# One GpSimd queue for all stores and zero fills, SyncE for loads alone, and more homes for w_mod tiles in a decode layer's forward and backward

## The chip, the core, the metric

The kernel runs on one core of a Trainium2 chip. A core has five engines that run on their own (TensorE for matmuls, VectorE, ScalarE, GpSimd, SyncE) and 16 DMA engines between HBM and the on-chip memory. The metric is the device time of one execution in microseconds; smaller is better. The runs come from several chips; the kernel before, run beside each group of them, took 719.1 to 720.5 us in the median, so times from different chips may be compared to within about 1 us.

## The reference

A decode layer for one token: adaptive layernorm, attention over a window of 4096 cached keys, a gated feed-forward, and the gradients of all of it.

```python
mod = (silu(c) @ w_mod).reshape(1, 6, 1, 1024)      # sa, ca, ga, sb, cb, gb
h = layernorm(x) * (1 + ca) + sa
x = x + ga * attention(h, k_cache[last 4096 of 65536], v_cache[same], wq, wo)
h = layernorm(x) * (1 + cb) + sb
x = x + gb * ((sigmoid(h @ w_gate) * (h @ w_up)) @ w_down)
# returned: x, and the gradients of x, k_cache, v_cache, wq, wo, w_gate, w_up, w_down, c, w_mod
```

With one token, each weight gradient is an outer product as large as its weight. The gradients of the two caches cover all 65536 positions, of which 61440 are zero: 120 MiB of zeros, written in 120 transfers of 1 MiB ("zero fills"). So 265.7 MB move, 186 of them written, and the arithmetic is small.

## The kernel before

Everything lives in one on-chip arena. Weight tiles are changed in place: VectorE reduces a tile against a broadcast gradient, then an outer product overwrites the tile, then the tile is stored. A tile's place is free for the next load only when its store has landed.

Zero fills go out on GpSimd's queue and are paced: each is tied to some result, so that they spread over the run.

```python
def zero(n, after=None):
    for _ in range(n):
        if not zleft:
            return
        ins = nc.gpsimd.dma_start(out=zleft.pop(0), in_=zeros[:, :])
        if after is not None:
            dep(ins, after)                 # wait for that result
```

The feed-forward (FFN) loop, seven blocks, five places for tiles ("slots"):

```python
def slot(i):
    return ar(F_OFF + 8 * (i % 5), 8)
wd_t = [slot(3 * n) for n in range(NB)]       # w_down; w_up: 3n+1; w_gate: 3n+2
...                                           # (cut)
for n in range(NB):
    ...                                       # (cut) gate and up matmuls (they need wu, wg), sigmoid,
    ...                                       # dhh = wd . b1k, ffn matmuls, dug, broadcast to du_b, dg_b
        outer_dve(wd[:, jj, :], hh[:, jj:jj + 1], b1k)
    nc.sync.dma_start(out=wd_dram(out_8, n), in_=wd_t[n])
    for j in range(KD):
        ttr(wu[:, j, :], wu[:, j, :], du_b, dh2acc[:, n * 16 + j:n * 16 + j + 1])
        last = outer_act(wu[:, j, :], h2[:, j:j + 1], du_b)
    nc.scalar.dma_start(out=dwu_view[:, :, n * FB:(n + 1) * FB], in_=wu)
    zero(1, last)
    if n + 1 < NB:
        if n + 1 > 1:
            load_wd(n + 1)
        load_wu(n + 1)
    ...                                       # (cut) the same for wg, stored by ScalarE, zero(1, last)
    if n + 1 < NB:
        load_wg(n + 1)                        # its slot is wd's of this block
```

A tile of w_up or w_gate is 128 partitions by 8 rows of 1 KB ("narrow rows"); w_down tiles and zero fills have rows of 8 KB. In the attention backward, w_mod is loaded again in eight tiles, into only two places:

```python
def sec_tile(j):
    return ar(F_OFF + 24 + 8 * (j % 2), 8)
```

## Time and profile before

| | before |
|---|---|
| time, median of 3 runs (lowest to highest) | 719.91 us (718.37 to 722.34) |
| span of the profiled run | 718.1 us |
| DMA busy, mean of 16 engines | 93% (42.2 + 37.9 + 13.1 + 0.2) |
| VectorE / ScalarE / TensorE / GpSimd busy | 43 / 29 / 21 / 9% |
| mean FFN block (first to seventh gate matmul, divided by 6) | 30.7 us |

One more part of the page is the DMA queues: packets, megabytes, and the share of the 16 engines' time that their packets took. q0 is GpSimd's queue, q1 SyncE's, q10 ScalarE's.

```profile
q0 software_dynamic: 17280, 125.84, 42.2%
q1 hardware_dynamic: 29920, 103.82, 37.9%
q10 hardware_dynamic: 21136, 35.66, 13.1%
```

The reader is to see the ratio of bytes to packets: GpSimd's queue moves 125.84 MB in 17280 packets, 7.3 KB each (8 KB and some for signalling), while ScalarE's moves 1.7 KB a packet, as two thirds of its packets are narrow rows (14336 of 1 KB).

### The profile page before, as it was taken

To read this page: it belongs to the slowest core of one execution; us is meant where nothing else is said; L and a number is where in the kernel's file an instruction comes from. 1 tells how busy PE (TensorE), PEld (TensorE's weight loads), DVE (VectorE), ACT (ScalarE), POOL (GpSimd) and SP (SyncE) were. 2 spreads that over 40 slices of the span, in tenths; PEclk is the share of its full clock that TensorE was granted. 3 is DMA by queue.
4 is the path that set the end of the run, shared out by engine and by line. 5 is a ranking of instruction groups with operands and counts; after the bars stand their busy time and mean duration, and the time that the engine had idled before them with its cause. 6 is when DMAs were issued, how large, how long until landed. Compare 5 with 4: busy or idle time off the path is not lost.

```text
span 718.1 us, 6808 instructions
## 1 busy us (share of the span) xinstructions
PE 148.1 (21%) x2648; PEld 125.4 (17%) x2648; DVE 309.3 (43%) x610; ACT 208.7 (29%) x298; POOL 66.1 (9%) x128
## 2 busy tenths in 40 slices
PE   2221226651220110201011100407714220000000
PEld 2221214551220110201011100106513120000000
DVE  2000003600236828356381899403994363200676
ACT  1000004610115606154260772445713230000026
POOL 2001101120100000000000021102100110000000
PEclk9999999965555555555555555556555555555555
DMA  8999999999969788797968699999999999997896
GB/s 347 428 426 425 427 425 427 416 421 416 417 251 377 273 321 309 270 365 249 381 209 325 241 412 422 398 407 419 416 420 425 413 418 417 412 422 281 323 384 270
DMA packets 68367, 265.74 MB, mean 370 GB/s; under 512 B 4208, under 2 KB 32880, under 8 KB 43120
## 3 DMA queue, kind: packets, MB, share of 16 engines
q0 software_dynamic: 17280, 125.84, 42.2%
q1 hardware_dynamic: 29920, 103.82, 37.9%
q10 hardware_dynamic: 21136, 35.66, 13.1%
q8 instruction: 20, 0.33, 0.2%
q14 instruction: 11, 0.09, 0.0%
HBM read 79.70 MB, written 185.60 MB: 369 GB/s over the span
## 4 chain that ended last, share of the span: by engine, by line
DMA 69%; DVE 16%; PE 6%; ACT 5%; issue 2%; SPq 1%; ACTq 1%; DVEq 0%
DMA out_dram<-arena 25%; DMA arena<-in_B_w_gate_dram 19%; DMA arena<-in_w_mod_dram 8%; DVE arena L151 8%; DMA arena<-in_A_wq_dram 6%; DMA arena<-in_A_k_cache_dram 5%; DMA arena<-in_A_wo_dram 4%; ACT arena L155 4%; DVE junk L151 2%; DVE arena L147 2%; PE tp_kv L309 2%; PE bc_ps L208 1%; ACT arena L312 1%; PE gu_ps L440 1%; DVE mx L330 1%
## 5 line engine op out<-in xcount | busy, mean ns | idle before, releaser
L151 DVE CUSTOM_DVE_ANT_0 arena<-arena 128x4096 bf16<-128x4096 bf16 (+1 forms) x24 | 88.5, 3709 | 97.0 <-DMA arena<-in_w_mod_dram 96.8
L119 POOL DMA_DIRECT2D out_dram<-zeros x120 | 65.0, 543 | 627.8 <-ACT arena L155 148.1
L440 PE MATMUL gu_ps<-h_bf,arena 128*128 128x1 bf16 x448 | 16.9, 172 | 152.0 <-DMA arena<-in_B_w_up_dram 102.5
L155 ACT ACTIVATE arena<-arena,cs_col 128x2048 bf16<-128x2048 bf16 x8 | 16.0, 2002 | 108.9 <-DVE dcs L151 106.4
L155 ACT ACTIVATE arena<-b1k,o_col 128x1024 bf16<-128x1024 bf16 x32 | 34.4, 1138 | 38.3 <-issue 15.5
L312 ACT COPY arena<-tp_kv 128x1024 bf16<-128x1024 bf16 x13 | 13.1, 1010 | 106.7 <-PE tp_kv L309 106.7
L440 PEld LDWEIGHTS <-arena 128*128 128x128 bf16 x448 | 16.0, 117 | 154.1 <-issue 131.5
L134 DVE TENSOR_TENSOR hh<-sg,gu_ps 128x4 f32<-128x4 f32 x7 | 1.1, 158 | 88.3 <-ACT om L445 88.3
L151 DVE CUSTOM_DVE_ANT_0 arena<-arena,b1k 128x1024 bf16<-128x1024 bf16 x32 | 36.7, 1217 | 0.0
L151 DVE CUSTOM_DVE_ANT_0 arena<-arena,du_b 128x512 bf16<-128x512 bf16 x56 | 34.8, 686 | 3.1 <-ACT du_b L473 3.1
L155 ACT ACTIVATE arena<-dg_b,h 128x512 bf16<-128x512 bf16 x56 | 35.0, 708 | 3.7 <-DVE dh2acc L151 3.7
L155 ACT ACTIVATE arena<-du_b,h 128x512 bf16<-128x512 bf16 x56 | 34.9, 710 | 0.0
L151 DVE CUSTOM_DVE_ANT_0 arena<-arena,dg_b 128x512 bf16<-128x512 bf16 x56 | 34.8, 685 | 0.0
L151 DVE CUSTOM_DVE_ANT_0 junk<-arena,b1k 128x1024 bf16<-128x1024 bf16 x28 | 34.2, 1222 | 0.5
L444 ACT ACTIVATE sg<-gu_ps 128x4 f32<-128x4 f32 x7 | 1.2, 173 | 93.3 <-PE gu_ps L440 93.3
L613 ACT ACTIVATE arena<-ps_kv 128x512 bf16<-128x512 f32 x32 | 16.1, 627 | 41.6 <-DMA out_dram<-arena 40.7
L309 PE MATMUL tp_kv<-ident_bf,arena 128*128 128x128 bf16 x256 | 22.3, 254 | 23.5 <-DMA arena<-in_A_k_cache_dram 15.6
L143 DVE COPY arena<-tp_kv 128x1024 bf16<-128x1024 bf16 x19 | 13.0, 690 | 31.0 <-PE tp_kv L309 31.0
L162 PE MATMUL rp_dc<-ident_f,dcv 128*8 128x128 f32 x1 | 0.4, 377 | 123.1 <-DVE dcv L134 123.1
L607 PE MATMUL ps_kv<-Q_hd,arena 8*128 8x128 bf16 x128 | 16.1, 295 | 41.6 <-ACT arena L613 41.6
L309 PEld LDWEIGHTS <-arena 128*128 128x128 bf16 x256 | 19.4, 116 | 26.3 <-DMA arena<-in_A_k_cache_dram 16.5
L162 PEld LDWEIGHTS rp_dc<-ident_f,dcv 128*8 128x8 f32 x1 | 0.1, 84 | 123.5 <-DVE dcv L134 123.5
(171 smaller groups left out, 336.3 us busy)
## 6 DMA issues: line engine op xcount, KB each, us to landing
out_dram<-zeros POOLq DMA_DIRECT2D x120, 1024.0 KB, 18.1
out_dram<-arena ACTq DMA_DIRECT2D x30, 1024.0 KB, 19.0
out_dram<-arena SPq DMA_DIRECT2D x23, 1024.0 KB, 18.7
arena<-in_A_wq_dram SPq DMA_DIRECT2D x15, 1024.0 KB, 40.4
arena<-in_w_mod_dram SPq DMA_DIRECT2D x8, 1536.0 KB, 26.9
arena<-in_A_wo_dram SPq DMA_DIRECT2D x8, 1024.0 KB, 37.7
arena<-in_w_mod_dram SPq DMA_DIRECT2D x8, 1024.0 KB, 5.8
arena<-in_B_w_down_dram SPq DMA_DIRECT2D x7, 1024.0 KB, 9.1
```

Source lines behind the costliest of these rows:

```text
L119: ins = nc.gpsimd.dma_start(out=zleft.pop(0), in_=zeros[:, :])
L143: return nc.vector.tensor_copy(out=out, in_=a)
L147: return nc.vector.tensor_scalar(out=out, in0=a, scalar1=s1, scalar2=None, op0=op0)
L151: return nc.vector.tensor_tensor_reduce(out=out, in0=w, in1=b, scale=1.0, scalar=0.0, op0=ALU.mult, op1=ALU.add, accum_out=acc)
L155: return nc.scalar.activation(out=out, in_=b, func=ACT.Copy, scale=col)
L208: nc.tensor.matmul(ps[:, jj * P:(jj + 1) * P], lhsT=col_bf[:, j0 + jj:j0 + jj + 1].broadcast_to([P, P]), rhs=ident_bf[:, :], start=(jj == ...
L309: nc.tensor.transpose(tp[:, t8 * P:(t8 + 1) * P], src[:, g, t_ * DH:(t_ + 1) * DH], ident_bf[:, :])
L312: last = nc.scalar.copy(out=o, in_=tp[:, :])
L330: nc.vector.reduce_max(out=mx8[:, ch:ch + 1], in_=P_bf[:, ch * 512:(ch + 1) * 512], axis=AX.X)
L440: nc.tensor.matmul(gu[:, half * 4 + jj:half * 4 + jj + 1], lhsT=w[:, j, jj::4], rhs=h2_bf[:, j:j + 1], start=(j == 0), stop=(j == KD - 1))
L607: nc.tensor.matmul(ps[:, t4 * DH:(t4 + 1) * DH], lhsT=rows[32 * g:32 * g + HG, t_ * P:(t_ + 1) * P], rhs=hd[32 * g:32 * g + HG, :], start= ...
L613: last = nc.scalar.activation(out=o, in_=ps[:, :], func=ACT.Copy, scale=float(scale))
```

## The change

The intent: no transfer should wait in the middle of a queue of another kind. All stores and zero fills go to GpSimd in one fixed order; SyncE only loads; ScalarE issues no transfers. (Exceptions of a few KB: three output vectors still leave by SyncE, and ScalarE still loads three input vectors at the start.) In the FFN loop each store is followed by two zero fills, so 42 are written there in place of 21, and w_down and w_up are loaded a block earlier. In the backward, each of the eight w_mod tiles (and of the eight half-size ones) has a place of its own in memory that has become free.

```diff
+    ZF = [(2, 2, 2)] * NB          # zero fills behind the wd, wu, wg store of a block
+    ZW_ = [1, 1, 1, 1, 1, 1, 1, 6] # behind the wo stores; ZS w_mod, ZQ wq, ZK k/v, ZT end
...
     load_wd(1)
+    load_wu(1)
...
-        last = cp(dug_bf, dug)
-        zero(1, last)
...
-        nc.sync.dma_start(out=wd_dram(out_8, n), in_=wd_t[n])
+        nc.gpsimd.dma_start(out=wd_dram(out_8, n), in_=wd_t[n])
+        zero(ZF[n][0])
...
-        nc.scalar.dma_start(out=dwu_view[:, :, n * FB:(n + 1) * FB], in_=wu)
-        zero(1, last)
-        if n + 1 < NB:
-            if n + 1 > 1:
-                load_wd(n + 1)
-            load_wu(n + 1)
+        nc.gpsimd.dma_start(out=dwu_view[:, :, n * FB:(n + 1) * FB], in_=wu)
+        zero(ZF[n][1])
...
-        nc.scalar.dma_start(out=dwg_view[:, :, n * FB:(n + 1) * FB], in_=wg)
-        zero(1, last)
+        nc.gpsimd.dma_start(out=dwg_view[:, :, n * FB:(n + 1) * FB], in_=wg)
+        zero(ZF[n][2])
         if n + 1 < NB:
             load_wg(n + 1)
+        if n + 2 < NB:
+            load_wd(n + 2)
+            load_wu(n + 2)
...
-    def sec_tile(j):
-        return ar(F_OFF + 24 + 8 * (j % 2), 8)
+    sec_off = [F_OFF + 24, F_OFF + 32, A_OFF + 56, C_OFF + 16, C_OFF + 24, B_OFF, B_OFF + 8, B_OFF + 16]
+    sec_t = [ar(o, 8) for o in sec_off]
+    s2_off = [B_OFF + 24, B_OFF + 28, F_OFF + 24, F_OFF + 28, F_OFF + 32, F_OFF + 36, A_OFF + 56, A_OFF + 60]
...            # (cut) all stores of the backward to nc.gpsimd with zero fills behind them, loads moved up,
...            # k/v gradient tiles alternate between two places, outputs of x and x2 moved to the end
```

More of the change, by code (lines that the diff above doesn't have):

```diff
@@ L113, in dep @@
                           reason="pace")
+    ZF = [(2, 2, 2)] * NB
+    ZW_ = [1, 1, 1, 1, 1, 1, 1, 6]
+    ZS = [1, 1, 1, 1, 1, 1, 1, 1]
+    ZQ = [1, 1, 1, 1, 1, 1, 1, 1]
+    ZK = [0, 0, 1, 0, 1, 0, 1, 0]
+    ZT = [0] * 7 + [99]
     def zero(n, after=None):
@@ L341, with transpose_rows @@
     zero(2, last)
-    def transpose_rows(src, name):
+    def transpose_rows(src, name, engs="AVAV"):
         dst = pool.tile([P, KT, G, HG], BF16, name=name, tag="pTdsT")
@@ L351, in transpose_rows @@
             i = tp[:, :].rearrange("p (t g r) -> p t g r", t=8, g=G)[:, :, :, 0:HG]
-            if tb % 2 == 0:
+            if engs[tb] == "A":
                 nc.scalar.copy(out=o, in_=i)
@@ L512 @@
     last = mulv(dmod_bf[:, 16:24], dx1, attn_col)
-    zero(4, last)
+    zero(2)
     dS = ar(F_OFF, 8)
@@ L520, with sec, s2_load @@
     dcs = vt([P, 2 * KD], "dcs")
-    def sec_tile(j):
-        return ar(F_OFF + 24 + 8 * (j % 2), 8)
+    sec_off = [F_OFF + 24, F_OFF + 32, A_OFF + 56, C_OFF + 16, C_OFF + 24, B_OFF, B_OFF + 8, B_OFF + 16]
+    sec_t = [ar(o, 8) for o in sec_off]
+    s2_off = [B_OFF + 24, B_OFF + 28, F_OFF + 24, F_OFF + 28, F_OFF + 32, F_OFF + 36, A_OFF + 56, A_OFF + 60]
+    s2_t = [ar(o, 4) for o in s2_off]
     def sec_load(j):
-        nc.sync.dma_start(out=sec_tile(j), in_=wm_view[:, j, 2048:6144])
-    def sec_ttr(j):
-        ttr(sec_tile(j), sec_tile(j), dmod_b4, dcs[:, j:j + 1])
-    def sec_outer(j, eng):
-        if eng == "A":
-            last = outer_act(sec_tile(j), cs_col[:, j:j + 1], dmod_b4)
-        else:
-            last = outer_dve(sec_tile(j), cs_col[:, j:j + 1], dmod_b4)
-        nc.sync.dma_start(out=dwm_view[:, j, 2048:6144], in_=sec_tile(j))
-        return last
+        nc.sync.dma_start(out=sec_t[j], in_=wm_view[:, j, 2048:6144])
+    def sec(j, nz):
+        ttr(sec_t[j], sec_t[j], dmod_b4, dcs[:, j:j + 1])
+        outer_dve(sec_t[j], cs_col[:, j:j + 1], dmod_b4)
+        nc.gpsimd.dma_start(out=dwm_view[:, j, 2048:6144], in_=sec_t[j])
+        zero(nz)
+    def s2_load(j):
+        nc.sync.dma_start(out=s2_t[j], in_=wm_view[:, j, 0:2048])
     sec_load(0)
     sec_load(1)
+    bcast(dmod_bf[:, 16:48], 32, dmod_b4, "A")
     do_col = vt([P, HQ], "do_col")
@@ L549 @@
             ttr(w, w, dattn_b, do_col[:, h:h + 1])
-            last = outer_act(w, o_col[:, h:h + 1], dattn_b)
-        nc.scalar.dma_start(out=dwo_view[:, q4 * 4:(q4 + 1) * 4, :], in_=wo_t[q4])
-        zero(2, last)
-    x2 = vt([P, KD], "x2")
-    mulv(x2, gb, ffn)
-    addv(x2, x2, x1)
-    col_to_row_out(x2, out_0[0], "x2")
-    for j in range(1, KD):
-        nc.sync.dma_start(out=wq_t[j], in_=wq_view[:, j, :])
+            outer_act(w, o_col[:, h:h + 1], dattn_b)
+        nc.gpsimd.dma_start(out=dwo_view[:, q4 * 4:(q4 + 1) * 4, :], in_=wo_t[q4])
+        zero(ZW_[q4])
+        if q4 < 7:
+            nc.sync.dma_start(out=wq_t[q4 + 1], in_=wq_view[:, q4 + 1, :])
+    sec_load(2)
     do_col2 = vt([P, 2 * HQ], "do_col2", BF16)
@@ L578 @@
                              tile_position=(0, 32 * g))
-        last = nc.vector.scalar_tensor_tensor(out=dS[:, ch * 512:(ch + 1) * 512], in0=ps[:, :], scalar=crow[:, 0:1],
-                                              in1=P_bf[:, ch * 512:(ch + 1) * 512], op0=ALU.subtract, op1=ALU.mult)
-    zero(2, last)
-    dsT = transpose_rows(dS, "dsT")
+        nc.vector.scalar_tensor_tensor(out=dS[:, ch * 512:(ch + 1) * 512], in0=ps[:, :], scalar=crow[:, 0:1],
+                                       in1=P_bf[:, ch * 512:(ch + 1) * 512], op0=ALU.subtract, op1=ALU.mult)
+    sec_load(3)
+    sec_load(4)
+    dsT = transpose_rows(dS, "dsT", "AAAA")
     DO_hd = make_hd(do_col2, "DO_hd")
-    bcast(dmod_bf[:, 16:48], 32, dmod_b4, "A")
+    sec(0, ZS[0])
     dq_ps, mm = av_like(k_nat, dsT, "dq")
-    zero(2, mm)
+    sec_load(5)
+    sec_load(6)
+    sec_load(7)
     dq_bf = vt([P, HQ], "dq_bf", BF16)
     ts(dq_bf, dq_ps[:, 0:HQ], SCALE, ALU.mult)
-    last = bcast(dq_bf, HQ, dq_b, "AV")
-    zero(2, last)
+    bcast(dq_bf, HQ, dq_b, "A")
+    sec(1, ZS[1])
+    for j in range(6):
+        s2_load(j)
     def kv_out(og, g):
@@ L596, with grad_kv @@
     gkv = []
-    for rows, hd, og, dst, scale in ((P_bf, DO_hd, out_3, x_T, None), (dS, Q_hd, out_2, k_nat, SCALE)):
+    for k, (rows, hd, og, scale) in enumerate(((P_bf, DO_hd, out_3, None), (dS, Q_hd, out_2, SCALE))):
         for g in range(G):
+            dst = ar(C_OFF + 8 * (g % 2), 8)
             for tb in range(KT // 4):
                 gkv.append((rows, hd, og, dst, scale, g, tb))
-    def grad_kv(items):
+    def grad_kv(items, nz):
         for rows, hd, og, dst, scale, g, tb in items:
@@ L608, in grad_kv @@
                                  rhs=hd[32 * g:32 * g + HG, :], start=True, stop=True, tile_position=(32 * g, 0))
-            o = dst[:, g, tb * 512:(tb + 1) * 512]
+            o = dst[:, tb * 512:(tb + 1) * 512]
             if scale is None:
-                last = nc.scalar.copy(out=o, in_=ps[:, :])
+                nc.scalar.copy(out=o, in_=ps[:, :])
             else:
-                last = nc.scalar.activation(out=o, in_=ps[:, :], func=ACT.Copy, scale=float(scale))
+                nc.scalar.activation(out=o, in_=ps[:, :], func=ACT.Copy, scale=float(scale))
             if tb == KT // 4 - 1:
-                nc.scalar.dma_start(out=kv_out(og, g), in_=dst[:, g, :])
-                zero(1, last)
+                nc.gpsimd.dma_start(out=kv_out(og, g), in_=dst)
+                zero(nz)
     dh1 = vt([P, KD], "dh1")
@@ L622 @@
         ttr(wq_t[j], wq_t[j], dq_b, dh1[:, j:j + 1])
-        grad_kv(gkv[8 * j:8 * j + 8])
-        last = outer_dve(wq_t[j], h1[:, j:j + 1], dq_b)
-        nc.sync.dma_start(out=dwq_view[:, j, :], in_=wq_t[j])
-        zero(1, last)
-        if j % 2 == 1 and j < 6:
-            k = j // 2
-            sec_ttr(k)
-            last = sec_outer(k, "V")
-            zero(1, last)
-            sec_load(k + 2)
+        outer_dve(wq_t[j], h1[:, j:j + 1], dq_b)
+        nc.gpsimd.dma_start(out=dwq_view[:, j, :], in_=wq_t[j])
+        zero(ZQ[j])
+        grad_kv(gkv[8 * j:8 * j + 8], ZK[j])
+        if j % 2 == 1:
+            sec(2 + j // 2, ZS[2 + j // 2])
+            if j == 1:
+                s2_load(6)
+                s2_load(7)
     dln1 = vt([P, KD], "dln1")
     mulv(dln1, dh1, ca1)
+    cp(dmod_bf[:, 0:8], dh1)
+    mulv(dmod_bf[:, 8:16], dh1, ln1)
+    dmod_b2 = dS[:, 0:2048]
+    bcast(dmod_bf[:, 0:16], 16, dmod_b2, "A")
     dx0b = layernorm_bwd_col(dln1, ln1, rstd1, "ln1b")
@@ L639 @@
     addv(dx0, dx0b, dx1)
-    cp(dmod_bf[:, 0:8], dh1)
-    last = mulv(dmod_bf[:, 8:16], dh1, ln1)
-    zero(2, last)
-    dmod_b2 = dS[:, 0:2048]
-    bcast(dmod_bf[:, 0:16], 16, dmod_b2, "A")
-    col_to_row_out(dx0, out_1[0], "dx0")
-    s2_t = [ar(C_OFF + 4 * j, 4) for j in range(KD)]
-    for j in range(KD):
-        nc.sync.dma_start(out=s2_t[j], in_=wm_view[:, j, 0:2048])
-    for k in range(3, KD):
-        sec_ttr(k)
-        last = sec_outer(k, "V")
-        zero(2, last)
-        if k + 2 < KD:
-            sec_load(k + 2)
-    zero(200, last)
+    col_to_row_out(dx0, out_1[0], "dx0")
+    x2 = vt([P, KD], "x2")
+    mulv(x2, gb, ffn)
+    addv(x2, x2, x1)
+    col_to_row_out(x2, out_0[0], "x2")
+    sec(6, ZS[6])
+    sec(7, ZS[7])
     for j in range(KD):
@@ L660 @@
         outer_act(s2_t[j], cs_col[:, j:j + 1], dmod_b2)
-        nc.scalar.dma_start(out=dwm_view[:, j, 0:2048], in_=s2_t[j])
+        nc.gpsimd.dma_start(out=dwm_view[:, j, 0:2048], in_=s2_t[j])
+        zero(ZT[j])
     t1 = vt([P, KD], "dc_t1")
```

## The prediction

> **What bounds the kernel now.** I read the page first: engine shares, the strip of 40 slices, the queues. No compute engine is above 43%, yet the DMA row is full for the first ten slices and again from slice 23 on.
>
> ```profile
> span 718.1 us, 6808 instructions
> PE 148.1 (21%) x2648; PEld 125.4 (17%) x2648; DVE 309.3 (43%) x610; ACT 208.7 (29%) x298; POOL 66.1 (9%) x128
> ...
> DMA  8999999999969788797968699999999999997896
> GB/s 347 428 426 425 427 425 427 416 421 416 417 251 377 273 321 309 270 365 249 381 209 325 241 412 422 398 407 419 416 420 425 413 418 417 412 422 281 323 384 270
> DMA packets 68367, 265.74 MB, mean 370 GB/s; under 512 B 4208, under 2 KB 32880, under 8 KB 43120
> ```
>
> The 265.74 MB are the same before and after: the change moves transfers, it removes none. At 414 GB/s, the rate of a full stretch, they alone would need 642 us. The kernel loses time where the DMA row is not full. So the next view is busy time by stretch, cut at the stages: first half; gap before the feed-forward (FFN) loop; FFN loop; attention backward; end. The last two columns are the busy share of the DMA engines and GB/s.
>
> ```profile
> 0.00:197.50 197.50, 62.36 (x1365) 55.32 (x1365) 30.11 (x77) 29.59 (x35) 24.22 (x50) 0.86 1.00 416
> 197.50:214.60 17.10, 4.48 (x104) 3.98 (x104) 5.38 (x16) 1.15 (x3) 0.61 (x1) 0.50 0.60 245
> 214.60:409.00 194.40, 26.59 (x624) 23.94 (x624) 113.04 (x333) 84.20 (x136) 10.61 (x19) 0.50 0.83 301
> 409.00:639.00 230.00, 54.33 (x554) 42.09 (x554) 124.84 (x156) 77.71 (x118) 27.51 (x52) 0.52 1.02 414
> 639.00:718.10 79.10, 0.38 (x1) 0.08 (x1) 35.96 (x32) 16.01 (x8) 3.16 (x6) 0.50 0.84 324
> ```
>
> Idle DMA time: 0.40 x 17.1 = 6.8 us, 0.17 x 194.4 = 33.0 us, 0.16 x 79.1 = 12.7 us; 52.5 us in all. Why it is idle in the FFN loop, the chain in order of time shows, one block of seven:
>
> ```profile
> 278.75 17.54 DMA arena<-in_B_w_gate_dram
> 296.42 1.22 PE gu_ps L440 x32
> ...
> 298.29 1.13 DVE junk L151
> 299.46 1.22 DVE junk L151
> ...
> 301.79 1.28 DVE arena L147 x3
> 303.09 6.64 DMA out_dram<-arena
> 309.80 17.53 DMA arena<-in_B_w_gate_dram
> ```
>
> A block lasts 31.05 us (278.75 to 309.80): 6.7 us of compute from the arrival of the gate weights to the store of the w_down tile, 6.64 us of that store, whose slot the next gate load takes, and 17.53 us of the load. The load is slow because SyncE issues the next w_down and w_up loads in the same moment, just ahead of it. DMA is then full for some 18 us and half idle for 13. Pacing ties three zero fills to events of each block, so nothing fills the hole:
>
> ```profile
> POOL out_dram L119 <- ACT arena L155: 148.1, 22, 17.1
> POOL out_dram L119 <- DVE dug_bf L143: 117.1, 7, 18.4
> ...
> SPq L476 <- DVE arena L147: 146.3, 7, 22.9
> SPq L526 <- DMA out_dram<-arena: 120.7, 8, 28.7
> ```
>
> GpSimd's zero fills wait for ScalarE and VectorE results (total, times, longest), and SyncE waits 146.3 us for computed tiles it is to store, and 120.7 us to load w_mod into the only two tiles it has, until their stores have landed. These two waits are what the change goes for.
>
> **What the Trainium skill says.** (1) "DMA: Bandwidth & Descriptors", section "Issuing engines are not separate DMA queues": all issuers share 16 engines; spreading over issuers saves only issue time. The trace agrees: 409 to 639 us runs at 414 GB/s with three queues. Moving the stores to GpSimd is no bandwidth change in itself. (2) Same page, "Queues, rings and completion order": each engine takes turns between queues packet by packet. So the lone load queue keeps a share however long GpSimd's backlog; no line here isolates it. (3) "SBUF — State Buffer", section "SBUF: two separate sides": GpSimd cannot write descriptors while VectorE holds the shared port in its fast modes. The 120 zero issues took 531 ns minimum and median, 1216 ns maximum, so this costs little here. (4) "DMA: Bandwidth & Descriptors", section "Specifications", gives about 358 GB/s as the HBM limit for a core; this trace holds 428 and I use the trace.
>
> **The change part by part.** Unit: 1 MiB = 1.049 MB.
>
> *Until 214.6 us* nothing moves except one more w_up load, so the gap stays: zeros behind the first w_down store now wait for it. Moved before: 197.5 x 416 + 17.1 x 245 = 86.3 MB; after: 87.4 MB. Left: 178.3 MB.
>
> *FFN loop.* Each block now stores 3 tiles and writes 6 zero regions in place of 3, all in GpSimd's order; 21 MiB of zeros come forward. The gate load goes first on SyncE, and w_down and w_up are fetched a block earlier. DMA work: 7 x 9 = 63 MiB out, 21 - 5 = 16 MiB in, together 79 MiB = 82.8 MB. The up and gate matrices go in rows of 1 KB, which are slower. From the row 214.6 to 409: 194.4 x 0.83 = 161 busy us for 194.4 x 301 = 58.5 MB; about 26 MiB (27.3 MB) of it in 1 KB rows. If the other 31.2 MB ran at 414 (75 us), these took 86 us: an estimate of 317 GB/s. A full sub-stretch at 378 GB/s suggests about 345; I take 330. After: 25 MiB (26.2 MB) in 1 KB rows, 79 us; 56.6 MB at 414, 137 us; together 216 us. Is it then DMA that binds? The chain would be 6.7 us compute, about 2.5 us for an unqueued store (1 MiB at 414) plus 2 us landing (estimate), then about 10 us for the gate load sharing with the stores: 21 us a block, against 216/7 = 31 us of transfers. The 10 us in hand are taken up by GpSimd's queue. So the loop gets no shorter (194 us before, about 216 for its bytes), but its DMA row becomes full.
>
> *Attention backward and end.* Left: 178.3 - 82.8 = 95.5 MB; at 414, 231 us. It must be kept full. VectorE after the FFN: 32 x 1.15 (wo) + 8 x 5.7 (wq) + 8 x 5.7 (w_mod) + 8 x 2.2 + some 15 of small work = 161 us, 70 below the DMA's 231, and with eight homes for the w_mod tiles its loads no longer wait for the store of the tile before last. Key and value gradients now alternate between two tiles instead of eight, so ScalarE waits for the store two back; about eight transfers, 20 us, stand behind that store, while refilling takes 4 us (8 x 0.5). Hidden.
>
> *End.* From the landing of the sixth gradient store: ScalarE's last eight copies (5 us), broadcast and layernorm (6), two w_mod tiles (11.4), the eight narrow tiles (18 + 4) make 44 us of compute. Behind it stand 21 MiB, 53 us of writes. The end stays covered; 12.7 us of idle become about 3.
>
> *Sum:* 214.6 + 216 + 231 + 3 = 665 us of span; the time is 1.9 above the span (719.98 against 718.1): 667. I round down to 665, since the narrow-row rate is the pessimistic end once more wide rows run beside it.
>
> **The rivals.**
> (a) Head-of-line blocking: in one static order a store whose tile is not ready holds every zero fill behind it, and the DMA row keeps its holes. For it: this queue waits 148 and 117 us today. Against: the 10 us in hand per block and the backlog of up to eight transfers (each GpSimd DMA in the new order waits for the eighth before it). If the holes stay at half their size: 665 + 20 = 685. If wholly: 710 to 720.
> (b) GpSimd's descriptor work becomes the bound: a zero fill has 128 rows at 531 ns; an up or gate store has 1024. If time goes with rows (estimate) that is 4.2 us, 14 times, plus 8 x 2.1 for the 512-row wo stores and some 150 others at 0.53: 156 us in total, 13 us of a 31 us block. Not a bound unless a row costs over twice that; then 690 to 700.
> (c) The writes on one queue run slower than when spread over three, as loads end some 100 us before the end. At 390 over 100 us it costs 6 us: 671.
> (d) Narrow rows cost less beside wide ones (400 in the loop): 207 instead of 216 us, 655.
>
> **Range and chances.** Best case, all full at 418 GB/s with the starting gap: 214.6 + 178.3/0.418 = 641. I put 8 in 10 on 648 to 692: (d) below, (a) in half or (b) above. Faster by over 2% means below 705.5; only (a) nearly whole or something unseen prevents it: 0.91. Within 2%: 0.06. Slower: 0.03.
>
> **What would show it.** In the strip of slices, the DMA row should be 9 from the FFN's first store to the last slice or two; one narrow hole at about 208 us remains. The FFN blocks should stand 29 to 32 us apart, GpSimd's longest waits should turn into waits for its own earlier transfers, and the attention-backward stretch should shrink by about 21 MiB (53 us at 414). The chain should be nearly all DMA. I am wrong if the DMA share in the loop stays below 0.95 (rival a), if an up or gate store holds GpSimd for over 8 us (b), if full stretches fall below 400 GB/s late in the run (c), or if the last 40 us are again half idle behind VectorE.

## The result

A ratio is the mean time of one kernel's fast runs over that of the other's fast runs of the same rounds, so it is not quite the ratio of the medians quoted.

| | before | after |
|---|---|---|
| time, median | 719.14 us (4 runs) | 680.27 us (4 runs, 679.51 to 681.59) |
| ratio | | 0.9462, 95% interval 0.9415 to 0.9509 |
| same again, on another chip | 720.04 us (11 runs) | 680.82 us (6 runs), 0.9454, 0.9424 to 0.9484 |
| span of the profiled run | 718.1 us | 678.8 us |
| mean FFN block | 30.7 us | 33.6 us |

The change gains 5.4%. The time lies in the predicted range, 15 us above the predicted 665. The page of the changed kernel, first its strip of slices and then its queues:

```profile
span 678.8 us, 6836 instructions
...
DMA  8999999999997999799979995999999999999995
GB/s 341 427 426 427 427 425 427 417 420 421 415 409 306 384 413 414 289 380 418 412 292 394 419 370 187 401 414 400 403 417 417 424 423 427 422 421 416 413 397 204
DMA packets 55567, 265.74 MB, mean 391 GB/s; under 512 B 4208, under 2 KB 18544, under 8 KB 30320
...
q0 software_dynamic: 28880, 185.61, 66.9%
q1 hardware_dynamic: 26608, 79.70, 29.5%
```

The row of sevens and nines in the middle has fewer holes than before, but it still has them: slices 13, 17, 21 and 25 (306, 289, 292 and 187 GB/s), one in every fourth slice, so one in every 67 us, two FFN blocks. There are also 12800 packets fewer for the same bytes, which nobody had asked for.

The stretches of the changed kernel, cut at the same times as before where they allow it (the last two columns are the DMA share and GB/s):

```profile
0.00:197.50 197.50, 62.18 (x1365) 54.97 (x1365) 27.94 (x73) 28.24 (x34) 23.28 (x48) 0.86 1.01 415
197.50:214.60 17.10, 5.68 (x136) 5.21 (x136) 8.51 (x22) 3.96 (x7) 2.26 (x5) 0.50 0.78 315
214.60:409.00 194.40, 22.90 (x552) 21.23 (x553) 97.26 (x284) 71.36 (x117) 32.00 (x52) 0.50 0.96 378
409.00:430.00 21.00, 3.94 (x55) 3.19 (x54) 17.91 (x63) 12.89 (x21) 6.58 (x11) 0.50 0.68 253
430.00:639.00 209.00, 51.35 (x544) 39.97 (x541) 133.62 (x140) 76.63 (x120) 35.78 (x62) 0.53 1.01 416
639.00:678.80 39.80, 0.38 (x1) 0.08 (x1) 20.15 (x26) 16.01 (x8) 6.40 (x12) 0.50 0.79 317
```

Idle DMA time is now 0.22 x 17.1 + 0.04 x 194.4 + 0.32 x 21 + 0.21 x 39.8 = 26.6 us, against 52.5 us before. That is 25.9 of the 39.3 us that the span lost. The other 13.4 us are engine time, the time for which the DMA engines are busy with packets. The queues' shares give nearly the same split: 93.4% of 718.1 = 671 us before and 96.6% of 678.8 = 656 us after, 15 us less for the same bytes.

Where the holes come from, the chain in order of time shows. Two blocks, one fast, one slow:

```profile
217.69 9.66 DMA arena<-in_B_w_gate_dram
227.48 1.21 PE gu_ps L449 x32
...
232.45 1.68 DVE arena L155 x4
...
234.41 13.71 DMA out_dram<-arena
248.18 25.55 DMA arena<-in_B_w_gate_dram
273.87 1.22 PE gu_ps L449 x32
...
284.83 0.26 DVE arena L159
285.09 9.34 DMA arena<-in_B_w_gate_dram
```

The block that starts at 206.44 takes 21 us, the next one 46.4 us, and so on in turn. In the slow one the w_down store takes 13.71 us (GpSimd's queue holds a store and zero fills ahead of it, the last of which lands at 245.34 us) and the gate load 25.55 us. When that load has landed, all the writes that were queued beside it have drained too, and GpSimd, whose next item is the w_down store of the new block, has nothing that it may send until the block's 7 us of compute are done:

```profile
POOL out_dram L484 <- DVE arena L155: 132.1, 7, 32.0
...
POOL out_dram L127 <- DMA out_dram<-arena: 41.7, 19, 5.0
```

L484 is the w_down store; seven waits, 132.1 us, the longest 32.0. It is head-of-line blocking, the prediction's rival (a): zero fills that could be sent stand behind a store that is not ready. But GpSimd's waiting is not all idle DMA time: of the wait of 32.0 us before the store at 280.82, the DMA engines stood empty for some 4 us (277 to 281).

### The profile page after: what moved, and what is told of

The parts are those of the page before. It is cut to its first block, busy times and chain, and to the rows that moved or that the text cites. A ratio compares the mean times of both kernels' runs of the same rounds, so it can differ in the third digit from the quotient of the medians.

```text
span 678.8 us, 6836 instructions
## 1 busy us (share of the span) xinstructions
PE 146.4 (22%) x2648; PEld 124.7 (18%) x2648; DVE 305.4 (45%) x604; ACT 209.1 (31%) x304; POOL 106.3 (16%) x189
## 3 DMA queue, kind: packets, MB, share of 16 engines
q1 hardware_dynamic: 26608, 79.70, 29.5%
## 4 chain that ended last, share of the span: by engine, by line
DMA 75%; DVE 12%; ACT 5%; PE 3%; issue 2%; SPq 0%; POOL 0%; POOLq 0%; ACTq 0%; DVEq 0%
DMA out_dram<-arena 24%; DMA arena<-in_B_w_gate_dram 20%; DMA arena<-in_A_wo_dram 10%; DMA arena<-in_A_wq_dram 7%; DVE arena L159 6%; DMA arena<-in_A_k_cache_dram 6%; DMA out_dram<-zeros 5%; DMA arena<-in_w_mod_dram 4%; ACT arena L163 3%; DVE junk L159 2%; PE gu_ps L449 1%; DVE arena L155 1%; ACT du_b L481 1%; ACT arena L221 1%; PE bc_ps L216 1%
## 5 line engine op out<-in xcount | busy, mean ns | idle before, releaser
L159 DVE CUSTOM_DVE_ANT_0 arena<-arena 128x4096 bf16<-128x4096 bf16 (+1 forms) x24 | 88.4, 3707 | 22.6 <-DMA arena<-in_w_mod_dram 22.6
L621 ACT CAST arena<-ps_kv 128x512 bf16<-128x512 f32 x32 | 16.1, 692 | 75.3 <-DMA out_dram<-arena 75.3
L159 DVE CUSTOM_DVE_ANT_0 arena<-arena,b1k 128x1024 bf16<-128x1024 bf16 x32 | 36.7, 1218 | 0.0
L617 PE MATMUL ps_kv<-DO_hd,P_bf 8*128 8x128 bf16 x128 | 15.1, 277 | 76.1 <-ACT arena L621 75.3
L617 PEld LDWEIGHTS <-P_bf 8*128 8x128 bf16 x128 | 11.9, 123 | 79.3 <-issue 77.9
L484 POOL DMA_DIRECT2D out_dram<-arena x7 | 3.7, 534 | 132.1 <-DVE arena L155 132.1
```

What stands on the lines that cost most here:

```text
L159: return nc.vector.tensor_tensor_reduce(out=out, in0=w, in1=b, scale=1.0, scalar=0.0, op0=ALU.mult, op1=ALU.add, accum_out=acc)
L617: nc.tensor.matmul(ps[:, t4 * DH:(t4 + 1) * DH], lhsT=rows[32 * g:32 * g + HG, t_ * P:(t_ + 1) * P], rhs=hd[32 * g:32 * g + HG, :], start= ...
L621: nc.scalar.copy(out=o, in_=ps[:, :])
```

## The experiments

Eleven kernels that differ from the two, and the changed one again. "Changed kernel" is the one after the change.

### 1. What a narrow load gets beside other queues

A kernel of transfers alone, in eight stretches, each begun when the one before has landed. It computes nothing. Its output is wrong, which doesn't matter for the time. Its calls, put together on fewer lines:

```diff
+    load(nc.sync, 7)                      # 1 narrow loads alone
+    phase(); store(nc.scalar, 7)          # 2 narrow stores, ScalarE
+    phase(); store(nc.gpsimd, 7)          # 3 narrow stores, GpSimd
+    phase(); zero(8)                      # 4 zero fills
+    phase(); zero(8); load(nc.sync, 3)    # 5
+    phase(); store(nc.gpsimd, 8); load(nc.sync, 3)   # 6
+    phase(); store(nc.scalar, 8); load(nc.sync, 3)   # 7
+    phase(); zero(8); load(nc.sync, 2); load(nc.scalar, 2)   # 8
```

> A wrong result on purpose: transfers alone, in eight stretches, each starting when the one before has landed. Turn-taking theory: a DMA engine takes one packet of each queue in turn, and a packet is one 1 KB row for a load or store from SyncE or ScalarE, but 4 KB for a narrow store from GpSimd (the packet counts of the two kernels say so) and 8 KB for a zero fill. Then: 7 MiB of narrow loads alone 20 to 22 us (about 355 GB/s), narrow stores from ScalarE the same, narrow stores from GpSimd 17.5 to 19 us (about 410), zero fills 424 GB/s. Three narrow loads beside eight zero fills: the first load lands only after some 20 us or more, because each of its 1024 rows waits for one 8 KB packet; beside eight narrow GpSimd stores after 13 to 15 us; beside eight narrow ScalarE stores after 6 to 7 us. With two load queues beside zero fills both first loads land at some 24 to 27 us. Rival, the queues share bytes evenly: the first load lands after 5 to 6 us in all of these.

The stretches where all queues of a phase were active, phases 1 to 6, two stretches of 7, then 8 (in the second of 7, from 180 us, the loads had landed and the stores ran alone; columns: VectorE, GpSimd, clock, DMA share, GB/s):

```profile
4.00:22.00 18.00, 14.99 (x9) 0.00 (x0) 1.00 1.10 351
28.00:44.00 16.00, 0.00 (x0) 0.00 (x0) 1.00 1.04 341
54.00:70.00 16.00, 0.00 (x0) 0.42 (x1) 1.00 1.01 334
78.00:94.00 16.00, 0.00 (x0) 0.00 (x0) 1.00 1.01 414
102.00:122.00 20.00, 0.00 (x0) 0.00 (x0) 1.00 1.02 422
136.00:150.00 14.00, 0.00 (x0) 0.00 (x0) 1.00 1.04 405
164.00:176.00 12.00, 0.00 (x0) 0.00 (x0) 1.00 1.09 386
180.00:190.00 10.00, 0.00 (x0) 0.00 (x0) 1.00 1.09 386
202.00:222.00 20.00, 0.00 (x0) 0.00 (x0) 1.00 1.03 417
```

Counting the packet records of the trace in those stretches gives each queue's part:

```
phase  beside the narrow load            packets: other / load       load gets
5      zero fills (8 KB packets)              905 / 1007             52 of 422 GB/s
6      narrow stores, GpSimd (4 KB packets)  1096 / 1146             84 of 405 GB/s
7      narrow stores, ScalarE (1 KB packets) 2267 / 2259            193 of 386 GB/s
8      zero fills and a second load queue     797 / 888 and 886      45 and 45 of 417 GB/s
```

The packet counts are within 12% of one to one in every case, whatever the sizes. With the packets of 4 bytes that signal the end of a transfer counted too, they are equal to within 0.4%: 1017 and 1015, 1161 and 1162, 2299 and 2291, 902, 902 and 904. The queues take turns by packet, not by byte, so a narrow load beside zero fills gets about an eighth of the bandwidth. The landings agree: the second load of a phase landed 20.7 us after the first beside zero fills, 10.4 beside GpSimd's narrow stores and 5.4 beside ScalarE's. A second load queue brings the loads from 52 to 90 GB/s together. This is what the Trainium skill's page "DMA: Bandwidth & Descriptors", section "Queues, rings and completion order", states (turns at packet granularity); the numbers are new. The same page's section "SWDGE vs HWDGE vs iDMA" says that GpSimd's path prefers packets of up to 4096 B. For narrow rows the runs agree: a narrow store from GpSimd is 256 packets of 4 KB, from ScalarE 1024 of 1 KB. But a zero fill, also from GpSimd, goes in packets of 8 KB.

Two parts of the expectation failed. Narrow stores from GpSimd alone ran at 334 GB/s, not 410: alone, into a tensor of the same shape, larger packets gained nothing over ScalarE's 341. (Into another tensor, at the end of phase 7, ScalarE's narrow stores alone ran at 386, so there is no one figure for them.) And the landing of the first load could not be used, as the loads began some us ahead of the zero fills.

### 2. More zero fills in the loop, nothing else

The kernel before with two fills at each of the three events of a block.

```diff
-        zero(1, last)      # three places in the FFN loop
+        zero(2, last)
```

> The kernel before with six zero fills per feed-forward block in place of three, still paced; nothing else of the change. If bringing zero fills forward into the holes of the loop were the whole of the gain: 680 us. Turn-taking theory: the holes fill, but the gate load, which takes turns with more 8 KB packets, slows and a block grows from 31 to 33 or 34 us; afterwards 21 MiB less are left, but the end still waits for the two w_mod tiles and has no zero fills left to cover it: 690 to 705 us.

It became slower: 740.99 us, ratio 1.0302 (1.0273 to 1.0330). The mean block grew from 30.7 to 39.8 us, more than expected. Its chain in order of time, one block:

```profile
249.16 10.53 DMA out_dram<-arena
259.77 22.79 DMA arena<-in_B_w_gate_dram
...
282.70 1.21 PE gu_ps L440 x32
```

The w_down store takes 10.53 us in place of 6.64 and the gate load 22.79 in place of 17.53. Between 262 and 274 us the packet records show 476 zero-fill packets, 534 narrow ones of SyncE and 532 of ScalarE: turns again. So zero fills brought forward are no gain in themselves; put into a loop whose loads come late, they cost more than they fill.

### 3. Fewer zero fills in the changed loop

```diff
-    ZF = [(2, 2, 2)] * NB
+    ZF = [(1, 1, 1)] * NB
-    ZW_ = [1, 1, 1, 1, 1, 1, 1, 6]
+    ZW_ = [3, 3, 3, 3, 3, 3, 3, 8]
-    ZK = [0, 0, 1, 0, 1, 0, 1, 0]
+    ZK = [1, 1, 1, 1, 1, 1, 1, 1]
```

> The changed kernel with three zero fills per block in place of six (one behind each store); the 21 others go behind the wo stores and the key and value gradients, where the DMA is full anyway. If the change gains by the zero fills that it brings into the loop: 695 us or more, as the loop is short of writes again. Turn-taking theory: less stands in the GpSimd queue, so the w_down store and the gate load come sooner and the loop's 12.6 MB blocks of 33.6 us become 9.4 MB blocks of about 25 us; the holes do not grow, and the time is 668 to 682 us, the same or a little better.

690.79 us, ratio 0.9577 (0.9539 to 0.9615): between the two expectations, so neither held. The mean block is 27.0 us, slower than the 25 expected: fast and slow blocks alternate here too (17.8 and 36.7 us). Against the changed kernel, seven blocks are 46 us shorter and the 21 MiB written later cost some 53 us at 416 GB/s. In the new loop, then, forward zero fills do pay, about 10 us of the 39, although they make its blocks longer; in the old one they cost 21.

### 4. The old loop in the new kernel

```diff
# FFN loop: stores, load order and paced zero(1, last) of the kernel before; the backward as changed
-    ZW_ = [1, 1, 1, 1, 1, 1, 1, 6]
+    ZW_ = [3, 3, 3, 3, 3, 3, 3, 8]
-    ZK = [0, 0, 1, 0, 1, 0, 1, 0]
+    ZK = [1, 1, 1, 1, 1, 1, 1, 1]
```

> The changed kernel with the whole feed-forward loop of before (its stores on SyncE and ScalarE, its load order, three paced zero fills per block); the static order and the w_mod homes stay in the attention backward. The loop then loses its 33 us of idle DMA time as before and the end is covered: 700 to 706 us. If the two parts only work together (the rest unable to take 21 MiB more of zero fills without delay): 715 or more. If the backward part is most of the gain: below 690.

712.11 us, ratio 0.9892 (0.9857 to 0.9926): the backward part alone is worth about 8 us, less than the 14 to 20 expected. (Its pieces were not tested apart; the eight places for w_mod are the likely one, as VectorE's idle time before its largest group, nearly all of it for w_mod loads, is 97.0 us on the page before and 22.6 on the page after.) Blocks are 31.0 us. With the run before this one it isolates the rest of the loop's change: both write three zero fills a block, and the new load order with the single queue is worth 712.11 - 690.79 = 21 us. The 39 us are thus 8 for the backward, 21 for the loop's order and 10 for the zero fills brought forward.

### 5. Stores on their own queue

The changed kernel with the FFN stores on ScalarE's queue and zero fills tied to results.

```diff
-        nc.gpsimd.dma_start(out=wd_dram(out_8, n), in_=wd_t[n])
-        zero(ZF[n][0])
+        nc.scalar.dma_start(out=wd_dram(out_8, n), in_=wd_t[n])
+        zero(ZF[n][0], last)
# and the same for the wu and wg stores
```

> The changed kernel with the feed-forward stores back on ScalarE's queue and the six zero fills of a block tied to ScalarE's and VectorE's results again; load order, slots and backward stay. If the single static queue matters only as an order, the w_down store now overtakes the zero fills and lands in 6 to 7 us in every block, and the loop gets shorter: 665 to 675 us. Turn-taking theory: with three queues a narrow load gets one turn in three, and the narrow stores are 1 KB packets again (14336 of them in place of 3584, 5 to 6 us of engine time): blocks of 34 to 38 us, 685 to 710 us.

683.01 us, ratio 0.9490 (0.9473 to 0.9508); the changed kernel had 0.9462 and 0.9454 on other chips, with overlapping intervals. The mean block is 34.1 us, as turn-taking has it, but the time is better than its 685 to 710. No alternation is left: each gate load takes about 18 us (18.68 and 17.89 in the first two blocks). So the single static queue itself is worth 2 us or nothing, all its effects taken together. It does save engine time: this run's queues took 97.3% of 681.4 = 663 us, the changed kernel's 656. By the packet records 5.8 of these 7 us are the 14 narrow stores (42.3 us in 1 KB packets, 36.5 in 4 KB), and 1.1 the narrow loads. No run let zero fills pass a store that was not ready with nothing else changed, so what head-of-line blocking costs by itself was not measured.

### 6. The gate load on a second queue, and the gate load late

The gate load is not the first in SyncE's queue: in the slow block the w_up load, issued at 240.39 us, finishes its packets only at 262.3, and the gate load, issued at 248.18, sends its own from then on. SyncE's issues:

```profile
240.39 0.37 SPq L426 DMA_DIRECT2D arena<-in_B_w_up_dram  x1
248.18 0.37 SPq L429 DMA_DIRECT2D arena<-in_B_w_gate_dram  x1
```

A second queue should let both take turns.

```diff
         if n + 1 < NB:
-            load_wg(n + 1)
+            nc.scalar.dma_start(out=wg_t[n + 1], in_=wg_view[:, :, (n + 1) * FB:(n + 2) * FB])
```

> The changed kernel with the gate loads issued from ScalarE, that is on a second load queue; nothing else. In the profile of the changed kernel the gate load of every second block takes 25 us, and some 15 of them go by while the w_up load ahead of it in SyncE's queue finishes. Turn-taking theory: both narrow loads then get turns at once, the slow block ends 4 to 8 us earlier, the mean block is about 31 to 32 us in place of 33.6, and the time 668 to 677 us. If the DMA bytes bound the loop: no change, 678 to 683 us.

715.87 us, ratio 0.9950 (0.9927 to 0.9973): a clear miss. Blocks took 39.9 to 40.9 us, the last 35.9 (mean 39.5). The run was confounded: ScalarE works in order, so it issued the gate load only when its last outer product was done (223.77 us in the first block, against 217.69). By then all stores and zero fills of the block stand in GpSimd's queue.

```profile
221.38 2.35 ACT arena L163 x4
223.77 22.64 DMA arena<-in_B_w_gate_dram
```

To part the two causes, the gate load stayed on SyncE but was held until that same moment:

```diff
-            load_wg(n + 1)
+            dep(load_wg(n + 1), last)     # last: ScalarE's last outer product of the block
```

> The changed kernel with the gate load still on SyncE's queue, but held until ScalarE's last outer product of the block, the moment at which the run with the gate on the second queue issued it. That run had no fast blocks any more: each took 40 us and its gate load 22.6 us, which is 64 turns (1024 packets over 16 engines) of 309 + 46 ns. If the late issue was the cause, and not the second queue: blocks of 37 to 42 us and 705 to 725 us. If the second queue was the cause: blocks stay near 33 us, 678 to 688 us.

701.55 us, ratio 0.9736 (0.9705 to 0.9767), mean block 36.8 us: just outside what the first theory asked for, far outside the second. Lateness explains 701.55 - 680.82 = 21 of the 35 us; the other 14 came with the second queue and are left open. (The 22.7 us worked out in the expectation fits the 22.64 by chance: in that load 4.5 us pass before the first packet, and 1024 packets then take 17.5 us.) What the run with the late load shows: the fast blocks exist because the gate load is issued the moment the w_down store lands, when little stands in the other queue. Six microseconds later costs 21 us in all.

### 7. Six slots

If a load need not wait for a store of the block before, the loop of store, load and compute is broken. A sixth place exists (wq's first tile, which is then loaded once more: 1 MiB).

```diff
-        return ar(F_OFF + 8 * (i % 5), 8)
+        return ar(F_OFF + 8 * ((i + 3) % 6), 8)
...
     load_wu(1)
+    load_wg(1)
...
-        if n + 1 < NB:
-            load_wg(n + 1)
         if n + 2 < NB:
             load_wd(n + 2)
             load_wu(n + 2)
+            load_wg(n + 2)
...
     sec_load(1)
+    nc.sync.dma_start(out=wq_t[0], in_=wq_view[:, 0, :])
```

> The changed kernel with six tiles for the feed-forward weights in place of five (the sixth is the place of one wq tile, which is loaded again later, 1 MiB or 2.5 us more), so that no load waits for a store of the block before. If the loop of store, load and compute causes the holes in the DMA row: they close, blocks of 30 to 31.5 us, 660 to 670 us. If the turns that narrow loads wait for are the whole bound of the loop: no gain, 680 to 684 us.

673.70 us, ratio 0.9354 (0.9321 to 0.9388), mean block 32.1 us: better than the changed kernel by about 7 us in spite of the extra MiB, but less than expected. The DMA row from 226 to 290 us is full (share 1.01); holes stay at the start of the loop and later. The alternation did not go: the gate matmuls now stand 8 and 56 us apart in turn, as each load waits for a store two blocks back and the loads of two blocks come together. Of the 33.6 us of a mean block the sixth place took away 1.5.

### 8. Zero fills of 4 KB

The direct test of turn-taking inside the kernel: same bytes, same order, same waits, half the packet size in the 42 zero fills of the loop.

```diff
+    def zero4k(n):
+        for _ in range(n):
+            nc.gpsimd.dma_start(out=zleft.pop(0).rearrange("p (a b) -> p a b", a=2),
+                                in_=zeros[:, 0:2048].unsqueeze(1).broadcast_to([P, 2, 2048]))
...
-        zero(ZF[n][0])        # and [1], [2]
+        zero4k(ZF[n][0])
```

> The changed kernel with the 42 zero fills of the feed-forward loop cut into 4 KB pieces in place of 8 KB; same bytes, same order, same waits. Turn-taking theory: a 1 KB packet of a load waits for 159 ns in place of 309, so the slow block's loads speed up; its 46.4 us become 38 to 43, the mean block 30 to 32 us, and the time 667 to 677 us in spite of some 1.5 us more engine time for the shorter packets. If bytes alone count: 680 to 684 us, blocks as before.

675.83 us, ratio 0.9397 (0.9372 to 0.9421), inside the first expectation and below the second's 680. The slow block shrank from 46.4 to 43.6 us (its gate load from 25.55 to 23.73), while the fast one grew from 21.0 to 22.4; over the whole loop slow blocks went from 46.3 to 44.5 us in the mean, and the mean block fell to 32.9 us. Both are above what was expected (38 to 43, and 30 to 32). The first slow block's store and gate load:

```profile
234.72 12.76 DMA out_dram<-arena
247.54 23.73 DMA arena<-in_B_w_gate_dram
```

The packets rose by 5376, 128 for each of the 42. Nothing but packet size differs, so the turns are a cause of the slow loads and not only a description of them; a small one here, of about 2 us in a load of 25. (The kernel's gain of 4 to 5 us is at the edge of the noise: its interval ends at 0.9421, and those of the changed kernel begin at 0.9415 and 0.9424.)

### 9. The last stores on SyncE

```diff
-        nc.gpsimd.dma_start(out=dwm_view[:, j, 0:2048], in_=s2_t[j])
-        zero(ZT[j])
+        nc.sync.dma_start(out=dwm_view[:, j, 0:2048], in_=s2_t[j])   # the two last zero fills now ahead
```

> The changed kernel with its last eight half-size w_mod stores on SyncE's queue, the last two zero fills ahead of them; nothing else. In the profile of the changed kernel some 4 us pass at the end in which half or fewer of the DMA engines work, and 3.8 us between the last data packet and the end of the span (1 us before the change). If the drain of GpSimd's queue is what makes this end: 3 to 6 us less than the changed kernel on the same chip, 674 to 678 us. If not: the same within 1.5 us.

677.18 us against the changed kernel's 680.82 on the same chip (ratios 0.9407, 0.9379 to 0.9436, and 0.9454, 0.9424 to 0.9484): 3.6 us less as expected, though the intervals overlap, so it is likely rather than shown. The changed kernel again, run beside it:

> The changed kernel itself, as the measure for the runs beside it on the same chip: 678 to 683 us.

680.82 us, as stated. The traces show how the end works. In the changed kernel the last zero fill lands at 674.93 us and the span ends 3.9 us later; for 3.1 of these GpSimd's closing DRAIN instruction goes on. With the last stores on SyncE, GpSimd's DRAIN ends before the last store lands, and the span ends 1.3 us after that landing. (The expectation's 3.8 is a reading of the same 3.9; counted from the last data packet, at 674.60, it is 4.2.) What did not go away is the stretch in which a part of the engines works: the DMA share stays below 0.65 for the last 6 us of packets in the changed kernel and for the last 7 in this one, so that is not a matter of GpSimd's queue alone.

### 10. Together

Six slots, zero fills of 4 KB in the loop, and the last stores on SyncE, in one kernel.

```diff
-        return ar(F_OFF + 8 * (i % 5), 8)
+        return ar(F_OFF + 8 * ((i + 3) % 6), 8)      # with the loads of experiment 7
-        zero(ZF[n][0])                               # and [1], [2]
+        zero4k(ZF[n][0])
-        nc.gpsimd.dma_start(out=dwm_view[:, j, 0:2048], in_=s2_t[j])
+        nc.sync.dma_start(out=dwm_view[:, j, 0:2048], in_=s2_t[j])
```

> Six weight tiles, zero fills of the loop in 4 KB pieces and the last stores on SyncE's queue, together. Each closes holes that the others leave in part, so less than the sum of the three: 664 to 671 us. If the loop is by now bound by bytes: 672 to 675 us, the loop gaining nothing over six tiles alone.

656.82 us, ratio 0.9121 (0.9092 to 0.9150), correct, and better than the best of the expectation. The strip and two stretches:

```profile
DMA  8999999999999899999999999999999999999996
GB/s 337 428 427 425 427 426 426 425 413 421 416 415 391 318 412 411 411 411 413 416 413 416 413 419 401 398 402 416 412 420 419 425 425 427 417 423 415 415 411 251
...
214.60:409.00 194.40, 31.17 (x645) 27.62 (x643) 119.91 (x355) 88.78 (x147) 46.83 (x65) 0.50 1.02 407
...
430.00:639.00 209.00, 50.27 (x513) 38.56 (x513) 129.00 (x122) 68.16 (x101) 36.39 (x60) 0.52 1.01 417
```

The DMA row is full from 230 us to the last slice, at 407 GB/s in the loop against 378 in the changed kernel (one slice at its start, 213 to 229 us, has 318). The mean block is 29.2 us: after a first pair of 8.1 and 47.3 us, the blocks no longer alternate (29.5 to 30.2). Alone, the three edits gained 7, 5 and 4 us; together 24. Each leaves a part of the loop's slack that the others use up: that reading is argued, not shown.

## Why the prediction was right, and where it was off

| run | blocks, mean us | time, us | ratio to before |
|---|---|---|---|
| before | 30.7 | 719.14 | 1 |
| more zero fills alone | 39.8 | 740.99 | 1.0302 |
| new backward alone | 31.0 | 712.11 | 0.9892 |
| new loop with 3 zero fills | 27.0 | 690.79 | 0.9577 |
| changed kernel | 33.6 | 680.27 | 0.9462 |
| six slots, 4 KB fills, last stores on SyncE | 29.2 | 656.82 | 0.9121 |

- **What bounds the kernel.** Right. (The strip was read one slice off: the DMA row before is full to slice 11, and again from 24 to 36.) The time is bytes over the DMA rate plus holes, and the gain is found in the DMA engines' time: 25.9 us of holes closed, 13.4 us of engine time saved, of which the prediction had only the first.
- **The stretch before the loop.** Right in kind: the gap stays (share 0.78 against 0.60).
- **The FFN loop.** This is the step that failed: "The chain would be 6.7 us compute, about 2.5 us for an unqueued store [...] plus 2 us landing (estimate), then about 10 us for the gate load". Fast blocks are like that (21.0 us, gate load 9.66, an unqueued store 4.2). Slow ones have 13.71 us of store and 25.55 us of load, because the store stands behind other writes, and the w_up load is ahead of the gate load in SyncE's queue and both take turns with 8 KB packets. The mean chain is 33.6 us, above the 31 us of transfers, so the "10 us in hand" were not there in every second block, and the DMA row did not become full (0.96, then 0.68 at its end; 0.92 from 206 to 430 us, below the 0.95 that the prediction named as its sign of being wrong). GpSimd's longest waits did not turn into waits for its own transfers either, but into those for the w_down tile (132.1 us). By 430 us, 166.1 MB had moved (the stretches' times multiplied by their rates), so 99.6 MB were left where 95.5 had been predicted: 4.1 MB, 10 us.
- **The narrow rows.** Taken at 330 GB/s, too slow. By their packets' time in the changed loop, loads of 1 KB packets ran at the equivalent of 349 GB/s on 16 engines (46.9 ns each) and the narrow stores, in 4 KB packets, at 404 (162 ns each): 69 us for the 25 MiB in place of 79. These 10 us have the other sign than the loop's 10 and about cancel them: that 665 came so close is in part luck.
- **Attention backward.** Right: 430 to 639 us at share 1.01 and 416 GB/s, for 414 predicted.
- **The end.** "12.7 us of idle become about 3": it was 8.4. VectorE and ScalarE were covered, as predicted (share 1.01 until 655 us). The idle time is the last 6 us of transfers, in which about half of the engines or fewer work, and the 3.9 us after the last landing (experiment 9).
- **The rivals.** (a) came true in part: with the slow chain it is found in the loop's 10 us, and the end's 5 us beyond the 3 predicted make up the rest of the 15; what the blocking alone costs was not measured. (b) is refuted: a narrow store took GpSimd 0.91 us, not 4.2. (c) is refuted: the late stretches hold 415 to 424 GB/s. (d) was true of the narrow rows' cost, as said above, and was hidden by the loop's waits.
- **What no step had.** The engine time. By the packet records, the stores that ScalarE issued with 1, 2 and 4 KB rows took 73.6 us of it before, and 68.4 after, all in 4 KB packets: 5 us of the 15. Another 8 are in the 8 KB packets: SyncE's lasted 338 ns in the mean before (400 in the loop, 309 to 310 before 180 us) and 311 after. Why they were longer is open.

## What to carry to other kernels

When several DMA queues are busy, count packets, not bytes: a load with 1 KB rows beside a queue of 8 KB packets gets about an eighth of the bandwidth, so what the next step waits for should be issued while the other queue is short, or perhaps have wide rows (not tried here). Filler writes delay the load that the loop waits for; they pay only where that costs less than the hole they fill: the same fills cost 21 us in one load order and gained 10 in another. And a single in-order queue saves little by itself (2 us or nothing here): the order of the loads with it (21 us) and one more buffer in the reuse chain (7 us) did more.

## What the Trainium skill lacked or had wrong

- "DMA: Bandwidth & Descriptors", section "Queues, rings and completion order": it gives packets of about 9 to 17 descriptors as typical. A narrow load or store from SyncE or ScalarE was one 1 KB row a packet here (1007 load packets against 905 of a zero fill in the same 20 us). The consequence, 52 of 422 GB/s for such a load, is on no page.
- Same page, section "Specifications": about 0.6 us to the first byte from SyncE or ScalarE. The first packet of a load came 1.0 to 1.1 us after issue with all queues empty (experiment 1), and 3.8 to 5.3 us after it for loads of the changed loop that were first in their queue while GpSimd's was busy.
- Same page, section "Specifications": about 358 GB/s as the HBM limit of a core, without a condition in that row; slices of these runs, of a program on one core, hold 424 to 428 GB/s. The same page's section "Bandwidth" does say that each core gets about 358 when both cores of a pair stream, so the row lacks its condition rather than being wrong.
- Same page, section "Issuing engines are not separate DMA queues": that another issuer saves only issue time leaves out, in that section, order and turns. A second load queue beside zero fills took the loads from 52 to 90 GB/s together; moving one load to another queue at the same moment cost 14 us (why is open).
- No page has the end of GpSimd's queue: 3.9 us from the last landing to the end of the span, 3.1 of them in GpSimd's DRAIN, against 1.0 us when ScalarE's stores came last (the kernel before).
